# An attention, MLP and mixture-of-experts kernel: weights ahead of keys and values in the opening, and two set-ups moved to the third weight quarter

## Chip, cores and metric

The kernel runs on one core of one Trainium2 chip. The metric is the device time of one execution in microseconds (us). A core has five engines that each work through a queue of their own in a fixed order: TensorE (PE: matrix products), VectorE (DVE), ScalarE (ACT), GpSimd (POOL), and SyncE (SP), which here only issues DMA transfers. They wait for each other by semaphores.

## The reference

```
kv  = einsum('bhsd,bhse->bhde', k, v)            # 8 batches, 8 heads, 576 positions, 64 wide
out = einsum('bhsd,bhde->bhse', q, kv)
x   = out / sqrt(mean(out*out, -1) + 1e-6) * g_norm      # 4608 tokens x 512
h   = x @ w_in                                   # w_in 512 x 2048
y   = (max(h, 0) + alpha * min(h, 0)) @ w_out    # w_out 2048 x 512
e   = argmax(y @ w_gate)                         # 8 experts; one per token
result = softmax(y @ w_gate)[e] * sigmoid(y @ w_output_gate)[e] * (relu(y @ w1[e]) @ w2[e])
```

The weights w_in, w_out, alpha and the two gate matrices arrive as inputs of the launch; w_in and w_out are 64-bit floats in memory, which the kernel reads as pairs of 32-bit integers.

## The kernel before

**Tiles and stages.** The 4608 tokens form 12 blocks of 3 tiles of 128 tokens. For each block the attention makes the three tiles of x; `h` multiplies x by w_in (16 groups f of 128 columns), ScalarE copies the product out scaled as `m`, VectorE applies alpha (`r`), ScalarE makes the 16-bit `g`, and `y` multiplies g by w_out. All products use 16-bit halves: a number is a high half plus a low half, so that each product is three matmuls. Afterwards a router (`l`) chooses each token's expert, and the rest of the program is the experts' products.

**The opening.** x needs kv, which needs all keys and values of a batch. `load_kv_first` fetches batch 0's k and v as two large transfers (into the room of later w_in tiles, which is why the profile names them wi), `load_q` a pair of query tiles; `kvps` are the key-value products, `qps`/`ops` the query transposes and products, and per tile t of block b a chain of small VectorE instructions ends in the line that writes the low half of x (L352 before, L354 after), whose transpose by DMA ("x<-x") TensorE's `h` waits for. The tiles of block 1 are tiles 3 to 5, so that its last is `x_0_5`.

**Weights while they arrive.** The first two blocks run through w_in and w_out in four quarters j, while the raw weights are loaded. A quarter of either matrix is GF = 4 raw tiles of 512 KB, and five raw tiles can be held at a time. Each is loaded (`Dense.load`, L414: `rawwi`, `rawwo`), then built to 32 bits (`Dense.build`: ScalarE's absolute value at L433, and on VectorE L434, L437, L439, L441), which also collects a maximum; when a quarter's four are built, `scale_in(j)` or `scale_out(j)` turns the maximum over all partitions into a power of two. That takes two small TensorE products (`all_max`: `allmaxwi`, `allmaxwo`, L132 and L137) with VectorE steps between and behind them, and then the tiles are split into the 16-bit halves (L455 on ScalarE, L456 on VectorE; `scol` and `sogs` are the scales, which depend on g_norm and alpha). A list `prep` holds these steps, and `prep_steps(n)` takes n of them at the places where the code calls it:

```
while prep:
    prep_steps(1)
    step(attq)
    step(attq)
drain(attq)
```

Here `step(attq)` takes one step of the attention of block 0 (first the four `kv_step`s of batch 0).

**What sets the order.** The code is handed to a scheduler that reorders each engine's instructions ahead of the run by its own estimate of the times, under the dependences; the order on every engine is then fixed. `tc.keep_in_program_order(t)` forbids it to place the instruction t on its engine ahead of those that the code wrote earlier. SP issues a DMA only when the one eight issues earlier has landed, so that at most eight are under way.

**Constants.** `lst` (the experts' token lists) is filled by eight transfers of a tile `dmy`; `wgr` holds both gate matrices, whose maximum `gam` gives a scale `swg`, and whose halves `wg16` the router uses.

Of the kernel before, what the change touches and what calls it, by code (L numbers as in the profile page):

```python
# [20 lines left out]
P = 128  # L21
# [38 lines left out]
def body(ctx: ExitStack, tc, q, k, v, g_norm, w_in, w_out, alpha, w_gate, w_og, w1, w2, out):  # L60
# [49 lines left out]
    def pow2(am, nm, out_s, out_inv, top=14, wide=False):  # L110


        e = small.tile([P, am.shape[1]], I32, tag="pw_e", name="pw_e" + nm, padded_shape=[P, E])
        dve.tensor_scalar(out=e, in0=am.bitcast(I32), scalar1=0x7FF00000 if wide else 0x7F800000, scalar2=None,
                          op0=ALU.bitwise_and)
        if wide:
            dve.tensor_scalar(out=e, in0=e, scalar1=float((896 + top + 1) << 20), scalar2=float((896 + 254) << 20),
                              op0=ALU.max, op1=ALU.min)
            dve.tensor_scalar(out=out_inv.bitcast(I32), in0=e, scalar1=8.0, scalar2=float(-((896 + top) << 23)),
                              op0=ALU.mult, op1=ALU.add)  # L120
        else:
            dve.tensor_scalar(out=out_inv.bitcast(I32), in0=e, scalar1=float((top + 1) << 23),
                              scalar2=float(-(top << 23)), op0=ALU.max, op1=ALU.add)
        dve.tensor_scalar(out=out_s.bitcast(I32), in0=out_inv.bitcast(I32), scalar1=-1.0, scalar2=float(254 << 23),
                          op0=ALU.mult, op1=ALU.add)
# [93 lines left out]
    def load_kv_first():  # L219
        for nm, src, w in (("k", k, wi[:, 6:11]), ("v", v, wi[:, 11:16])):  # L220
            t = w.rearrange("p a t f -> p (a t f)").bitcast(F32)
            m = t[:, 0:H * QJ * D].rearrange("p (h j d) -> p h j d", h=H, j=QJ)
            r = t[0:SR, H * QJ * D:H * (QJ + 1) * D].rearrange("p (h d) -> p h d", h=H)
            sp.dma_start(out=m, in_=src[0, :, 0:QJ * P, :].rearrange("h (p j) d -> p h j d", j=QJ))
            sp.dma_start(out=r, in_=src[0, :, QJ * P:S, :].rearrange("h p d -> p h d"))
            kv_in[nm + "r", 0] = r
            for n in range(NPAIR):
                kv_in[nm, n] = m[:, 2 * n:2 * n + 2]

    def kv_step(n):  # L230
        b, hp = kv_order[n]
        kk, vv = kv_in.pop(("k", n)), kv_in.pop(("v", n))
        kr, vr = kv_in["kr", b], kv_in["vr", b]

        if hp % 2 == 0:
            kv_ps[b] = ps_a.tile([P, 2, D], F32, tag="a", name=f"kvps_{b}_{hp}")
        ps = kv_ps[b]
        for j in range(QJ + 1):
            for i in range(2):
                x, y = (kr[:, 2 * hp + i, :], vr[:, 2 * hp + i, :]) if j == 0 else (kk[:, i, j - 1, :], vv[:, i, j - 1, :])  # L240
                pe.matmul(ps[64 * i:64 * i + 64, hp % 2, :], x, y, start=(j == 0), stop=(j == QJ))
        if hp % 2 == 1:
            for i in range(2):
                sl = slice(64 * i, 64 * i + 64)
                dve.tensor_copy(out=kvbd[b % 2][sl, hp - 1:hp + 1, sl], in_=ps[sl])
        load_kv(n + 2 if n >= NPAIR else n + NPAIR if n < 2 else len(kv_order))
# [142 lines left out]
    def split(dst_h, dst_l, src, s):  # L389
        act.activation(out=dst_h, in_=src, func=AF.Copy, scale=s)  # L390
        dve.scalar_tensor_tensor(out=dst_l, in0=src, scalar=s, in1=dst_h, op0=ALU.mult, op1=ALU.subtract)  # L391
# [161 lines left out]
    def step(gens):  # L553
        while gens:
            if next(gens[0], "end") != "end":
                return
            gens.pop(0)
# [478 lines left out]
    def load_next():  # L1036
        if order:
            d, i = order.pop(0)
            d.load(i)

    load_kv_first()
    load_q(0, True)
    for _ in range(5):
        load_next()
    load_q(1, True)
    for half in range(2):
        sp.dma_start(out=gp[64 * half:64 * half + 64, :], in_=g_norm.rearrange("(p o) -> p o", o=1))
    gm = small.tile([P, 1], F32, tag="amx", name="gm")
    dve.tensor_scalar(out=gm, in0=gp, scalar1=-1.0, scalar2=None, op0=ALU.mult)
    dve.tensor_tensor(out=gm, in0=gm, in1=gp, op=ALU.max)  # L1050
    pow2(all_max(gm, "g"), "g", sg, isg, top=0)
    dve.tensor_tensor(out=gp, in0=gp, in1=sg, op=ALU.mult)
    al = small.tile([NF, P], F32, tag="al", name="al")
    sp.dma_start(out=al, in_=alpha.rearrange("(f p) -> f p", p=P))
    alp = ps_l.tile([P, NF], F32, tag="l", name="alp")
    pe.transpose(alp, al, ident[:NF, :NF])
    dve.tensor_copy(out=alphat, in_=alp)
# [27 lines left out]
    def prep_out(j):  # L1085
        return ([partial(build, dout, i) for i in range(j * GF, (j + 1) * GF)] + [partial(scale_out, j)]
                + [partial(dout.split, i) for i in range(j * GF, (j + 1) * GF)])
# [3 lines left out]
    def prep_steps(n):  # L1091
        for _ in range(n):
            if prep:
                prep.pop(0)()

    while prep:
        prep_steps(1)
        step(attq)
        step(attq)
    drain(attq)  # L1100
    for load in late:
        load()
    late = None
    dmy = small.tile([P, RT], I32, name="dmy", bufs=1)
    pool.memset(dmy, DUMMY)
    for e in range(E):
        sp.dma_start(out=lst.rearrange("(e p c) o -> e p (c o)", e=E, p=P)[e], in_=dmy)

    wgr = small.tile([P, NC, 2, E], F32, tag="wgr", name="wgr", bufs=1)
    sp.dma_start(out=wgr[:, :, 0, :], in_=w_gate.rearrange("(c p) e -> p c e", p=P))  # L1110
    sp.dma_start(out=wgr[:, :, 1, :], in_=w_og.rearrange("(c p) e -> p c e", p=P))
    gam = small.tile([P, 1], F32, tag="amx", name="gam")
    dve.tensor_reduce(out=gam, in_=wgr.rearrange("p c t e -> p (c t e)"), axis=AX.X, op=ALU.max,
                      apply_absolute_value=True)
    swg = small.tile([P, 1], F32, tag="swg", name="swg")
    pow2(all_max(gam, "wg"), "wg", swg, kl)
    for c in range(NC):
        split(wg16[:, c, 0, :], wg16[:, c, 1, :], wgr[:, c].rearrange("p t e -> p (t e)"), swg)

    def h_then_attention(i):  # L1120
        emit_h_block(i)
# [11 lines left out]
    attq.append(att_steps(1))  # L1133
    for j in range(NG):
        prep.extend(prep_out(j))
        if j == 0:
            drain(attq)
            h_part(0, j, gts[0])
            prep_steps(len(prep))
            y_part(0, j, gts[0], accs[0])  # L1140
            drain(attq)
            prep.extend(prep_in(1))
            h_part(1, j, gts[1])
        else:
            h_part(0, j, gts[0])
            if j == NG - 1:
                xt.pop(0)
                attq.append(att_steps(2))
            h_part(1, j, gts[1])
            prep_steps(len(prep))  # L1150
            if j < NG - 1:
                prep.extend(prep_in(j + 1))
            if j == NG - 1:
                xt.pop(1)
            y_part(0, j, gts[0], accs[0])
        if j == NG - 1:
            yq.append(lambda: route_1(0, *first[0]))
        y_part(1, j, gts[1], accs[1])
        prep_steps(len(prep))
# [72 lines left out]
```

## Time and profile before

| what | value |
|---|---|
| three executions, median (lowest to highest) | 1452.66 us (1451.47 to 1453.32) |
| the profiled execution: its own time, and its span | 1451.28 us, 1449.5 us |
| its mean granted clock of TensorE | 0.958 of full speed |
| TensorE busy | 1323.1 us, 91% of the span |
| VectorE busy | 836.9 us, 58% |
| ScalarE busy | 568.1 us, 39% |
| GpSimd busy | 333.9 us, 23% |

The span runs from the first to the last record of the profile; what the execution's own time has beyond it is 1.8 us. A busy share is a mean over stages: in the first 100 us TensorE waits much, later it hardly does.

### The profile page before, as it was taken

How to read it: one execution, taken by the hardware profiler on the slowest of the kernel's cores; microseconds unless marked ns; L12 is line 12 of the kernel's file. 1: busy time of each engine (PE TensorE's matmuls, PEld its weight loads, DVE VectorE, ACT ScalarE, POOL GpSimd, SP SyncE). 2: the span in 40 equal slices, each digit the busy share in tenths (PEclk: the TensorE clock that was granted, in tenths of full speed). 3: DMA queues.
4: the chain of work that ended last, by engine and by line, in shares of the span. 5: the costliest groups of instructions: out<-in, count | busy, mean ns of one | idle time of the engine just before them, and what ended most of it. 6: DMA issues, size and time to landing. Idle time of an engine off the chain costs nothing. (4 is left out here: it accounts for less than half of the span.)

```text
span 1449.5 us, 22268 instructions
## 1 busy us (share of the span) xinstructions
PE 1323.1 (91%) x7586; PEld 678.5 (47%) x7586; DVE 836.9 (58%) x2428; ACT 568.1 (39%) x937; POOL 333.9 (23%) x329
## 2 busy tenths in 40 slices
PE   4679985799999989999999999999789979999998
PEld 3435543445555545555555555544334434443443
DVE  5999877668786968788786876535012111211221
ACT  3365543346464646555555555411111111111111
POOL 2023334122132422212122222021212211211211
PEclk9589997899999989999999999999999999999999
DMA  9944047668595747686856663169996897689774
GB/s 255 280 113 144 1 118 152 81 131 210 142 269 123 212 121 175 189 218 197 168 160 136 198 154 96 23 163 128 291 260 134 223 252 198 135 215 215 141 152 139
DMA packets 347571, 243.25 MB, mean 168 GB/s; under 512 B 267692, under 2 KB 300476, under 8 KB 342464
## 3 DMA queue, kind: packets, MB, share of 16 engines
q1 hardware_dynamic: 330528, 206.11, 60.8%
q0 software_dynamic: 7712, 18.92, 4.2%
q10 hardware_dynamic: 9216, 16.78, 3.5%
q8 instruction: 60, 0.98, 0.3%
q14 instruction: 55, 0.45, 0.1%
HBM read 248.86 MB, written 53.97 MB: 209 GB/s over the span
## 5 line engine op out<-in xcount | busy, mean ns | idle before, releaser
L581 PE MATMUL h<-x,wi 128*128 128x384 f16 x2304 | 418.3, 334 | 12.1 <-DMA x<-x 5.8
L600 PE MATMUL y<-wo,g 128*128 128x512 f16 x1728 | 407.8, 383 | 12.4 <-ACT g L588 7.2
L581 PEld LDWEIGHTS <-wi 128*128 128x128 f16 x2304 | 224.9, 100 | 173.4 <-issue 22.6
L600 PEld LDWEIGHTS <-g 128*128 128x128 f16 x1728 | 164.9, 98 | 196.4 <-issue 8.5
L1009 DVE CAST h_d<-br_d 128x512 f16<-128x512 f32 x74 | 31.8, 430 | 332.4 <-DMA hT_d<-h_d 234.3
L1003 PE MATMUL bh_d<-lane,byT_d 128*128 128x512 f16 x888 | 201.3, 383 | 10.2 <-DMA lane<-ws 10.2
L1024 PE MATMUL bo_d<-lane,hT_d 128*128 128x512 f16 x888 | 200.5, 383 | 10.2 <-DMA hT_d<-h_d 10.0
L588 ACT CAST g<-r 128x384 f16<-128x384 f32 x192 | 97.4, 509 | 131.6 <-DVE r L586 125.5
L1003 PEld LDWEIGHTS <-byT_d 128*128 128x128 f16 x888 | 87.5, 99 | 118.6 <-issue 16.6
L1024 PEld LDWEIGHTS <-hT_d 128*128 128x128 f16 x888 | 87.2, 99 | 118.7 <-DMA hT_d<-h_d 13.3
L586 DVE SCALAR_TENSOR_TENSOR r<-m,alphat 128x384 f32<-128x384 f32 x192 | 123.1, 642 | 22.6 <-ACT m L584 18.1
L329 POOL TENSOR_TENSOR rs<-ms,mhalf 128x8 f32<-128x8 f32 x36 | 67.4, 1874 | 226.7 <-DVE qm L332 223.2
L1007 ACT ACTIVATE br_d<-bh_d 128x512 f32<-128x512 f32 x74 | 44.2, 597 | 177.3 <-PE bh_d L1003 138.9
L584 ACT ACTIVATE m<-h,scal 128x384 f32<-128x384 f32 x160 | 91.6, 574 | 40.5 <-PE h L581 37.3
L589 DVE TENSOR_TENSOR g<-r,g 128x384 f16<-128x384 f32 x160 | 92.9, 582 | 24.0 <-ACT g L588 21.4
L391 DVE SCALAR_TENSOR_TENSOR wlo_w<-rawe,es_w,whi_w 128x1024 f16<-128x1024 f32 x64 | 85.4, 1349 | 27.6 <-ACT whi_w L390 17.3
L1027 ACT ACTIVATE ob_d<-bo_d,msc_d 128x512 f32<-128x512 f32 x37 | 25.4, 687 | 165.1 <-PE bo_d L1024 160.6
L390 ACT ACTIVATE whi_w<-rawe,es_w 128x1024 f16<-128x1024 f32 x64 | 71.2, 1142 | 42.7 <-DMA ws<-whi_w 22.6
L521 ACT ACTIVATE eab_w<-rawe 128x1024 bf16<-128x1024 f32 x64 | 67.2, 1056 | 49.5 <-DMA rawe<-in_moe_w_dram 46.1
L1028 POOL DMA_INDIRECT out_dram<-ob_d,idx_d x37 | 38.5, 1040 | 193.8 <-ACT ob_d L1027 163.6
L726 POOL DMA_INDIRECT lst<-ids,pos x36 | 37.5, 1041 | 171.7 <-DVE pos L723 107.6
L352 POOL TENSOR_TENSOR x<-xs,x 128x512 f16<-128x512 f32 x30 | 46.9, 1563 | 110.7 <-ACT x L351 81.9
(297 smaller groups left out, 1288.9 us busy)
## 6 DMA issues: line engine op xcount, KB each, us to landing
lane<-ws SPq DMA_DIRECT2D x150, 1024.0 KB
rawe<-in_moe_w_dram SPq DMA_DIRECT2D x64, 512.0 KB
ws<-whi_w ACTq DMA_DIRECT2D x64, 256.0 KB
ws<-wlo_w SPq DMA_DIRECT2D x64, 256.0 KB
ytab<-row SPq DMA_DIRECT2D x32, 256.5 KB
q<-in_q_dram SPq DMA_DIRECT2D x16, 512.0 KB
rawwi<-in_moe_w_in_dram SPq DMA_DIRECT2D x16, 512.0 KB
rawwo<-in_moe_w_out_dram SPq DMA_DIRECT2D x16, 512.0 KB
```

Source lines behind the costliest of these rows:

```text
L329: pool.tensor_tensor(out=rs, in0=ms, in1=mhalf, op=ALU.pow)
L390: act.activation(out=dst_h, in_=src, func=AF.Copy, scale=s)
L391: dve.scalar_tensor_tensor(out=dst_l, in0=src, scalar=s, in1=dst_h, op0=ALU.mult, op1=ALU.subtract)
L521: act.activation(out=ab.rearrange("p a b -> p (a b)"), in_=raws[4 * m + i], func=AF.Abs)
L581: pe.matmul(ps, wi[:, f // 4 * NC + c, w, fs], xt[i][:, xc, :], start=(n == 0), stop=(n == 3 * NC - 1))
L584: act.activation(out=r0, in_=ps, func=AF.Copy, scale=(scst if start else scal)[:, f:f + 1])
L586: dve.scalar_tensor_tensor(out=r, in0=r0, scalar=alphat[:, f:f + 1], in1=r0, op0=ALU.mult, op1=ALU.max)
L588: act.copy(out=hi, in_=r)
L589: (pool if start else dve).tensor_tensor(out=lo, in0=r, in1=hi, op=ALU.subtract)
L600: pe.matmul(ps, g[:, t, f % GF, us], wo[:, f, w, :], start=(start and m == 0), stop=(stop and m == 2))
L1003: pe.matmul(hp, j["yT"][:, x, :], w1_[:, w, c, hs], start=(m == 0), stop=(m == 3 * NC - 1))
L1024: pe.matmul(po, hT[:, g, :], w2_[:, w, f, :], start=(m == 0), stop=(m == 3 * NFE - 1))
```

## The change

Five things are moved. In the opening, the four raw tiles of the first quarter of w_in, then g_norm (`gp`) and alpha (`al`), are loaded ahead of keys, values and queries. Ahead of the first `kv_step`, the code now writes the four builds and `scale_in(0)`, and only the four splits remain for the loop, which takes one step of the attention per step of `prep` where it took two. The first key-value product is kept in program order on TensorE. The filling of the lists and the set-up of the gate weights become a function that is called at j == 2. And at j == 0 the attention of block 1 is no longer drained ahead of `h_part(0, 0, ...)`. No instruction's work is changed. Lines after L241 stand 2 lower down in the changed kernel, until L1040.

```diff
--- before.py
+++ after.py
@@ -238,7 +238,9 @@
         for j in range(QJ + 1):
             for i in range(2):
                 x, y = (kr[:, 2 * hp + i, :], vr[:, 2 * hp + i, :]) if j == 0 else (kk[:, i, j - 1, :], vv[:, i, j - 1, :])
-                pe.matmul(ps[64 * i:64 * i + 64, hp % 2, :], x, y, start=(j == 0), stop=(j == QJ))
+                t = pe.matmul(ps[64 * i:64 * i + 64, hp % 2, :], x, y, start=(j == 0), stop=(j == QJ))
+                if (n, j, i) == (0, 0, 0):
+                    tc.keep_in_program_order(t)
         if hp % 2 == 1:
             for i in range(2):
                 sl = slice(64 * i, 64 * i + 64)
@@ -1038,20 +1040,21 @@
             d, i = order.pop(0)
             d.load(i)
 
+    for _ in range(GF):
+        load_next()
+    for half in range(2):
+        sp.dma_start(out=gp[64 * half:64 * half + 64, :], in_=g_norm.rearrange("(p o) -> p o", o=1))
+    al = small.tile([NF, P], F32, tag="al", name="al")
+    sp.dma_start(out=al, in_=alpha.rearrange("(f p) -> f p", p=P))
     load_kv_first()
     load_q(0, True)
-    for _ in range(5):
-        load_next()
+    load_next()
     load_q(1, True)
-    for half in range(2):
-        sp.dma_start(out=gp[64 * half:64 * half + 64, :], in_=g_norm.rearrange("(p o) -> p o", o=1))
     gm = small.tile([P, 1], F32, tag="amx", name="gm")
     dve.tensor_scalar(out=gm, in0=gp, scalar1=-1.0, scalar2=None, op0=ALU.mult)
     dve.tensor_tensor(out=gm, in0=gm, in1=gp, op=ALU.max)
     pow2(all_max(gm, "g"), "g", sg, isg, top=0)
     dve.tensor_tensor(out=gp, in0=gp, in1=sg, op=ALU.mult)
-    al = small.tile([NF, P], F32, tag="al", name="al")
-    sp.dma_start(out=al, in_=alpha.rearrange("(f p) -> f p", p=P))
     alp = ps_l.tile([P, NF], F32, tag="l", name="alp")
     pe.transpose(alp, al, ident[:NF, :NF])
     dve.tensor_copy(out=alphat, in_=alp)
@@ -1093,29 +1096,31 @@
             if prep:
                 prep.pop(0)()
 
+    prep_steps(GF + 1)
     while prep:
         prep_steps(1)
-        step(attq)
         step(attq)
     drain(attq)
     for load in late:
         load()
     late = None
-    dmy = small.tile([P, RT], I32, name="dmy", bufs=1)
-    pool.memset(dmy, DUMMY)
-    for e in range(E):
-        sp.dma_start(out=lst.rearrange("(e p c) o -> e p (c o)", e=E, p=P)[e], in_=dmy)
-
-    wgr = small.tile([P, NC, 2, E], F32, tag="wgr", name="wgr", bufs=1)
-    sp.dma_start(out=wgr[:, :, 0, :], in_=w_gate.rearrange("(c p) e -> p c e", p=P))
-    sp.dma_start(out=wgr[:, :, 1, :], in_=w_og.rearrange("(c p) e -> p c e", p=P))
-    gam = small.tile([P, 1], F32, tag="amx", name="gam")
-    dve.tensor_reduce(out=gam, in_=wgr.rearrange("p c t e -> p (c t e)"), axis=AX.X, op=ALU.max,
-                      apply_absolute_value=True)
-    swg = small.tile([P, 1], F32, tag="swg", name="swg")
-    pow2(all_max(gam, "wg"), "wg", swg, kl)
-    for c in range(NC):
-        split(wg16[:, c, 0, :], wg16[:, c, 1, :], wgr[:, c].rearrange("p t e -> p (t e)"), swg)
+
+    def constants():
+        dmy = small.tile([P, RT], I32, name="dmy", bufs=1)
+        pool.memset(dmy, DUMMY)
+        for e in range(E):
+            sp.dma_start(out=lst.rearrange("(e p c) o -> e p (c o)", e=E, p=P)[e], in_=dmy)
+
+        wgr = small.tile([P, NC, 2, E], F32, tag="wgr", name="wgr", bufs=1)
+        sp.dma_start(out=wgr[:, :, 0, :], in_=w_gate.rearrange("(c p) e -> p c e", p=P))
+        sp.dma_start(out=wgr[:, :, 1, :], in_=w_og.rearrange("(c p) e -> p c e", p=P))
+        gam = small.tile([P, 1], F32, tag="amx", name="gam")
+        dve.tensor_reduce(out=gam, in_=wgr.rearrange("p c t e -> p (c t e)"), axis=AX.X, op=ALU.max,
+                          apply_absolute_value=True)
+        swg = small.tile([P, 1], F32, tag="swg", name="swg")
+        pow2(all_max(gam, "wg"), "wg", swg, kl)
+        for c in range(NC):
+            split(wg16[:, c, 0, :], wg16[:, c, 1, :], wgr[:, c].rearrange("p t e -> p (t e)"), swg)
 
     def h_then_attention(i):
         emit_h_block(i)
@@ -1133,8 +1138,9 @@
     attq.append(att_steps(1))
     for j in range(NG):
         prep.extend(prep_out(j))
+        if j == 2:
+            constants()
         if j == 0:
-            drain(attq)
             h_part(0, j, gts[0])
             prep_steps(len(prep))
             y_part(0, j, gts[0], accs[0])
```

On SP, in the first transfers of the program, before:

```order
L224 DMA wi<-in_k_dram 128x8x256
L225 DMA wi<-in_k_dram 64x8x64
L224 DMA wi<-in_v_dram 128x8x256
L225 DMA wi<-in_v_dram 64x8x64
L212 DMA q_0_193<-in_q_dram 128x8x128
L414 DMA rawwi_195<-in_moe_w_in_dram 128x1024
L414 DMA rawwi_197<-in_moe_w_in_dram 128x1024
L414 DMA rawwi_199<-in_moe_w_in_dram 128x1024
L414 DMA rawwi_201<-in_moe_w_in_dram 128x1024
L414 DMA rawwo_203<-in_moe_w_out_dram 128x1024
L212 DMA q_2_205<-in_q_dram 128x8x128
```

and now:

```order
L416 DMA rawwi_189<-in_moe_w_in_dram 128x1024
L416 DMA rawwi_191<-in_moe_w_in_dram 128x1024
L416 DMA rawwi_193<-in_moe_w_in_dram 128x1024
L416 DMA rawwi_195<-in_moe_w_in_dram 128x1024
L1046 DMA gp<-in_g_norm_dram 64x1 x2
L1048 DMA al<-in_moe_alpha_dram 16x128
L224 DMA wi<-in_k_dram 128x8x256
L225 DMA wi<-in_k_dram 64x8x64
L224 DMA wi<-in_v_dram 128x8x256
L225 DMA wi<-in_v_dram 64x8x64
L212 DMA q_0_205<-in_q_dram 128x8x128
L416 DMA rawwo_207<-in_moe_w_out_dram 128x1024
```

The four rawwi and the two small transfers went from behind k, v and the first q to the front of the queue; the first rawwo stands behind k, v and q as before.

On VectorE, around the last tile of block 1's x (`x_0_5`; `cwo`, `cwi` and `uwi` are steps of builds, `wi<-wo` and `wo<-wi` splits), before:

```order
L441 SCALAR_TENSOR_TENSOR wi<-rawwo_937,cwo_1141 128x512
L352 TENSOR_TENSOR x_0_4_689<-xs_4_672,x_0_4_689 128x512
L347 TENSOR_TENSOR xs_5_709<-ops_5_704,rs_5_715 128x512
L437 TENSOR_SCALAR cwo_1197<-uwo_1194 128x512
L441 SCALAR_TENSOR_TENSOR wi<-rawwo_965,cwo_1169 128x512
L117 TENSOR_SCALAR pw_ewo_1231<-pw_ewo_1231 128x1
L456 SCALAR_TENSOR_TENSOR wi<-wo,scol,wi 128x512 x2
L437 TENSOR_SCALAR cwi_1329<-uwi_1326 128x512
L456 SCALAR_TENSOR_TENSOR wi<-wo,scol,wi 128x512 x2
L439 SCALAR_TENSOR_TENSOR cwo_1197<-rawwo_993,cwo_1197 128x512
L352 TENSOR_TENSOR x_0_5_726<-xs_5_709,x_0_5_726 128x512
L119 TENSOR_SCALAR isog<-pw_ewo_1231 128x1
```

and now:

```order
L349 TENSOR_TENSOR xs_5_854<-ops_5_849,rs_5_860 128x512
L136 TENSOR_SCALAR amdiagwi_1365<-ident,amrowwi_1363 1x1
L458 SCALAR_TENSOR_TENSOR wi<-wo,scol,wi 128x512
L479 TENSOR_SCALAR sogs<-sgn,sog 128x4
L458 SCALAR_TENSOR_TENSOR wi<-wo,scol,wi 128x512
L485 TENSOR_TENSOR em<-em,eg 128x1
L458 SCALAR_TENSOR_TENSOR wi<-wo,scol,wi 128x512 x2
L114 TENSOR_SCALAR pw_ewi_1368<-allmaxwi_1361 128x1
L354 TENSOR_TENSOR x_0_4_834<-xs_4_817,x_0_4_834 128x512
L354 TENSOR_TENSOR x_0_5_871<-xs_5_854,x_0_5_871 128x512
L487 TENSOR_TENSOR egd_1204<-eg,em 128x1
```

Ahead of `x_0_5` there were 17 rows of L434 and 15 of L441, and there are now 25 of the former (L436 there) and 20 of the latter (L443); the two tiles x_0_4 and x_0_5, which stood nine rows apart, stand one behind the other.

On TensorE, where the maximum of the last quarter of w_out (`allmaxwo_1968`) is spread to all partitions, before:

```order
L581 MATMUL h_15_1921<-x_358,wi 128x384
L581 LDWEIGHTS wi
L581 MATMUL h_15_1921<-x_358,wi 128x384
L581 LDWEIGHTS wi
L581 MATMUL h_15_1921<-x_358,wi 128x384
L137 MATMUL allmaxwo_1968<-amdiagwo_1972,ones_70 128x1
L581 LDWEIGHTS wi
L581 MATMUL h_12_1947<-x_582,wi 128x384
```

and now:

```order
L602 MATMUL y_2_1_1721<-wo,g_176 128x512
L602 LDWEIGHTS g_176
L602 MATMUL y_2_1_1721<-wo,g_176 128x512
L602 LDWEIGHTS g_176
L602 MATMUL y_2_1_1721<-wo,g_176 128x512
L137 MATMUL allmaxwo_1968<-amdiagwo_1972,ones_70 128x1
L583 LDWEIGHTS wi
L583 MATMUL h_11_1663<-x_660,wi 128x384
```

That product stood behind the last `h` of block 0 (h_15), and it now stands ahead of h_11 of block 1, some 200 rows of the queue earlier.

## Rows read from the trace of the kernel before

**Rows 1.** The page: the span, and busy time by engine.

```profile
span 1449.5 us, 22268 instructions
...
PE 1323.1 (91%) x7586; PEld 678.5 (47%) x7586; DVE 836.9 (58%) x2428; ACT 568.1 (39%) x937; POOL 333.9 (23%) x329
```

**Rows 2.** Stretches: span, busy us of PE, PEld, DVE, ACT, POOL; clock; DMA share, GB/s.

```profile
15.50:98.40 82.90, 56.57 (x344) 37.77 (x344) 75.58 (x258) 39.40 (x70) 17.50 (x12) 0.71 0.80 208
...
18.00:20.00 2.00, 1.41 (x12) 0.89 (x8) 2.00 (x6) 0.87 (x2) 0.00 (x0) 1.00 1.04 375
...
30.00:32.00 2.00, 0.00 (x1) 0.00 (x0) 1.72 (x6) 1.49 (x3) 1.57 (x1) 1.00 0.30 41
```

**Rows 3.** SP's timeline, opening: start, duration, line, transfer issued.

```profile
6.90 4.02 SPq L414 DMA_DIRECT2D rawwi<-in_moe_w_in_dram  x4
10.96 0.43 SPq L414 DMA_DIRECT2D rawwo<-in_moe_w_out_dram  x1
...
12.34 5.06 SPq L1047 DMA_DIRECT2D gp<-in_g_norm_dram  x2
...
25.31 4.62 SPq L1107 DMA_DIRECT2D lst<-dmy  x6
```

**Rows 4.** ScalarE's timeline, opening; brackets: idle time before, and what ended it.

```profile
16.50 0.67 ACT L433 ACTIVATE uwi<-rawwi 128x512 f32<-128x512 f32 x1 [0.62 <-DMA rawwi<-in_moe_w_in_dram]
17.85 0.67 ACT L433 ACTIVATE uwi<-rawwi 128x512 f32<-128x512 f32 x1 [0.68 <-DMA rawwi<-in_moe_w_in_dram]
...
21.93 0.67 ACT L433 ACTIVATE uwo<-rawwo 128x512 f32<-128x512 f32 x1 [1.15 <-DVE cwi L437]
```

**Rows 5.** TensorE's timeline, opening.

```profile
12.46 5.91 PE L241 MATMUL kvps<-wi 64*64 64x64 f32 x80 [12.46 <-DMA wi<-in_v_dram]
...
68.04 1.48 PE L581 MATMUL h<-x,wi 128*128 128x384 f16 x4
...
101.50 8.76 PE L581 MATMUL h<-x,wi 128*128 128x384 f16 x36 [4.37 <-DMA x<-x]
```

**Rows 6.** VectorE's timeline: first work, one tile's build, block 1's last x.

```profile
15.57 0.59 DVE L245 COPY kvbd<-kvps 64x128 f32<-64x128 f32 x2 [12.83 <-PE kvps L241]
16.19 0.69 DVE L434 TENSOR_SCALAR_CACHE_REDUCE uwi<-uwi 128x512 f32<-128x512 f32 x1
...
17.38 0.69 DVE L439 SCALAR_TENSOR_TENSOR cwi<-rawwi,cwi 128x512 int32<-128x512 int32 x1
...
97.66 0.67 DVE L352 TENSOR_TENSOR x<-xs,x 128x512 f16<-128x512 f32 x1
```

**Rows 7.** TensorE's timeline around the last quarter of w_out.

```profile
197.65 0.59 PE L600 MATMUL y<-wo,g 128*128 128x512 f16 x2 [1.60 <-ACT wo L455]
198.65 2.16 PE L600 MATMUL y<-wo,g 128*128 128x512 f16 x6 [0.41 <-DVE wo L456]
200.61 3.13 PE L581 MATMUL h<-x,wi 128*128 128x384 f16 x12
...
206.16 2.11 PE L581 MATMUL h<-x,wi 128*128 128x384 f16 x12
```

**Rows 8.** ScalarE's timeline, the same place.

```profile
196.88 1.33 ACT L455 ACTIVATE wo<-rawwo,sogs 128x512 f16<-128x512 f32 x2 [2.44 <-DVE sogs L477]
```

**Rows 9.** TensorE's timeline behind it.

```profile
215.87 0.27 PE L132 MATMUL allmaxkv<-ident,kvam 128*8 128x128 f32 x1 [0.83 <-DVE kvam L254]
218.62 0.38 PE L137 MATMUL allmaxkv<-amdiagkv,ones 8*128 8x8 f32 x2 [2.48 <-DVE amdiagkv L136]
222.94 0.40 PE L676 MATMUL l<-wg,yT 128*128 128x32 f16 x8 [3.93 <-DMA yT<-row]
```

**Rows 10.** VectorE's timeline in that stretch.

```profile
205.05 4.56 DVE L524 TENSOR_TENSOR eam_w<-eam_w,eab_w 128x512 bf16<-128x512 bf16 x5
```

**Rows 11.** GpSimd's and TensorE's timelines, far from the opening.

```profile
496.49 9.08 POOL L352 TENSOR_TENSOR x<-xs,x 128x512 f16<-128x512 f32 x1 [6.90 <-ACT x L351]
...
514.87 2.31 PE L600 MATMUL y<-wo,g 128*128 128x512 f16 x5 [5.54 <-ACT g L588]
```

## The prediction

> **What bounds the kernel now.** Over the whole span TensorE is the bound: it is busy for 91% of 1449.5 us [rows 1]. The change lies in the first hundred microseconds, where that doesn't hold: between 15.5 and 98.4 TensorE is busy for 56.6 of 82.9 us and VectorE for 75.6 [rows 2]. So I read next what TensorE's opening waits for. Its key-value products begin at 12.46, when v has landed; its first product with w_in comes at 68.04; and block 1's first `h` at 101.50 has 4.4 us of idle time before it, ended by the transposed x [rows 5]. The instruction that makes this x is VectorE's at 97.66 [rows 6], and the transfer and its start take the 3.2 us behind it. From there to 196.05 TensorE's timeline shows no hole of a microsecond, so **the time of `x_0_5` sets when the dense part really starts**, and VectorE's queue sets `x_0_5`. The next hole is at 197.65: 1.60 us for a split of w_out's last quarter, and 0.41 for the next [rows 7]. Behind it come three larger ones, 0.83, 2.48 and 3.93 us, until the router's first product at 222.94 [rows 9]; the first two are released by VectorE, and the third by a transpose of what VectorE wrote.
>
> **Transfers.** The opening is limited by bandwidth: at 18 to 20 us the DMA engines are full with 375 GB/s [rows 2]. Raw tiles reach ScalarE 1.35 us apart, each awaited for 0.6 to 0.7 us [rows 4]. Four of them put ahead of k and v thus delay k, v and q by some 5.4 us, and the key-value products begin near 17.9. But keys, values, one pair of queries, four raw tiles of w_in and one of w_out are the same set in either order, so the first raw tile of w_out lands when it did. The third raw tile was there at 17.85, so the fifth, w_out's, at 17.85 + 2 × 1.35 = 20.6; ScalarE took it only at 21.93, after 1.15 us in which it waited for VectorE [rows 4]. VectorE's first step on it can thus begin at about 21.4. That step stands in VectorE's new order right behind the four builds and the scale, ahead of the first copy of a key-value product.
>
> **How much lead VectorE gains.** Now its first work is at 15.57, when the first key-value product is there [rows 6]. One build takes 1.2 us from L434 to L439, and L439 and L441 fill 0.6 each before the next can start [rows 6], together 2.4, or 2.2 where nothing is late. Four are 9.2; some thirty small steps for g_norm, alpha and the scale add 2.0. So 11.2 us of work lie ahead of 21.4. Whether VectorE starts them at 5 or at 8, it has finished before and waits. Before the change it had done 5.8 us of work by then (from 15.57). **The lead is 5.4 us**, not the ten that its first instruction moves.
>
> **What now stands ahead of x_0_5.** The order has 8 more L434, 6 more L437, 7 more L439 and 5 more L441 ahead of it, and four gate splits fewer. At 0.69, 0.4, 0.6 and 0.6 us, that is 5.5 + 2.4 + 4.2 + 3.0 = 15.1; four gate splits of 0.16 and smaller steps take 0.6 off: **14.5 us**. Against it stands the idle time inside the stretch, 82.9 − 75.6 = 7.3 us [rows 2]. Part of it comes from late raw tiles of w_out: SP spends 4.62 us at 25.31 on list fills that wait for earlier ones [rows 3], while the DMA engines carry 41 GB/s [rows 2]. In the new order the tiles of w_out stand ahead of the fills. I let 3.5 of the 7.3 us go, half of it; the ends are none and all. So x_0_5, and with it h of block 1, come 14.5 − 5.4 − 3.5 = **5.6 us later**, from 1.8 (no idle time left) to 9.1 (all of it left). This is the change's cost: VectorE does the builds of later quarters ahead of the x that TensorE waits for. The x of block 0 comes at about the same time as before, since its wait for the split of w_in is replaced by one for x.
>
> **What comes back.** The builds that were done early are missing later, so VectorE is further ahead by the last quarter. The product that spreads w_out's last maximum stands ahead of h_11 of block 1 instead of behind h_15 of block 0, so the scale that ScalarE awaited for 2.44 us at 196.88 [rows 8] is there early: **−2.0 us** (1.60 + 0.41), at worst 0. The twelve `h` behind that hole took 3.13 us at half clock, and twelve of the same kind 2.11 at 206.16 [rows 7]: **−1.0**, between 0 and −1.5.
>
> The Trainium skill (TensorE: Matmul & The Clock Gate, What's actually happening) has the clock fall after a stretch without activity. Two waits of 1.60 and 0.41 us with products between them are hardly such a stretch, and if by that rule the fall has another cause the 1.0 us would not come back; no other row here settles it.
>
> At 205.05 VectorE spends 4.56 us on five maxima of expert weights [rows 10], in front of the work on which the holes at 215.87, 218.62 and 222.94 depend. In the new order seven such steps stand earlier, where TensorE has enough to do: 5.5 us of VectorE's queue, against 7.2 us of holes [rows 9]. I take **−3.5**, between 0 and −5.5, because the first products in this stretch also wait for ScalarE and for transposes.
>
> The gate weights and lists cost nothing where they now stand: by order the fills remain among the opening's transfers, and the router needs the gate halves only at 222.94.
>
> **Sum.** 5.6 − 2.0 − 1.0 − 3.5 = −0.9 us on the profiled execution's 1451.28 us (1.8 over its span). It is 1.4 below the median of 1452.66, to which I apply the same difference: **1451.8 us**. The ends are 1.8 − 2.0 − 1.5 − 5.5 = −7.2 (1445.5) and +9.1 (1461.8). The measurement tells 0.2%, or 2.9 us, from no change.
>
> **Rivals.** *Nothing is given back* (slower). The delay of x_0_5 stays and the late gains don't come, since transposes and ScalarE's queue end the waits around 222 instead of VectorE: +5.6, 1458.3 us. It counts as slower once less than 2.7 us comes back. For it speaks that the 3.93 us hole ends with a DMA; against it that the transpose is issued only when VectorE's row is written.
>
> *VectorE has no gaps any more* (faster). With all 7.3 us of idle time gone, x_0_5 is only 1.8 late, and with the gains at their middle values the sum is 1.8 − 6.5 = −4.7, 1448.0 us. For it speaks that raw tiles now come in the order in which VectorE takes them; against it that several of its steps wait for TensorE's maxima, which stand between products of h and y.
>
> *A far hole moves* (faster). At 514.87 TensorE has 5.54 us of idle time, in a chain that goes back to one GpSimd instruction of 9.08 us at 496.49 [rows 11], long after the change. TensorE's order differs in places until about 550 us; if this meeting of instructions is broken up, the sum is −0.9 − 5.5 = −6.4, 1446.3 us. A new one could arise as well, so its chance is small.
>
> **Numbers.** The forecast (within 0.2%) gets 0.42, nothing given back 0.25, no gaps 0.23, the far hole 0.10. Faster is then 0.33, same 0.42, slower 0.25. A range from 1446 to 1459 holds the rivals' centres and leaves out the outermost ends, which need every bound at once.
>
> **What the profile after would show.** Right: VectorE's first build near 6 us, a wait of some microseconds before 21.4, key-value products at 17 to 19, block 1's first `h` at 103 to 111, no wait for a split of w_out near 197, and the row of the router's first product at most 2 us from 222.9. Wrong: if VectorE doesn't wait for w_out's tile (then the lead is up to 9 us), if a TensorE maximum stalls VectorE between 80 and 105, or if the key-value products, rather than builds, hold up VectorE after 22.

## The result, and the profile after

The changed kernel is slower: 1469.2 us median (1466.32 to 1471.42, 4 runs) beside 1452.99 (1451.47 to 1458.46), a ratio of 1.0096 with a 95% interval of 1.0072 to 1.012 (the quotient of the two medians, 1.0112, lies inside it). Forecast was 1451.8 us. The profiled execution took 1467.59 us; its page begins, against [rows 1], with

```profile
span 1465.9 us, 22269 instructions
...
PE 1312.9 (90%) x7586; PEld 673.8 (46%) x7586; DVE 843.8 (58%) x2428; ACT 569.7 (39%) x937; POOL 335.5 (23%) x329
```

so that its span is 16.4 us longer. TensorE's timeline of the changed kernel says where, against [rows 5, 9]:

```profile
19.90 5.91 PE L241 MATMUL kvps<-wi 64*64 64x64 f32 x80
...
77.22 6.89 PE L583 MATMUL h<-x,wi 128*128 128x384 f16 x24 [5.96 <-DMA x<-x]
...
116.42 6.09 PE L583 MATMUL h<-x,wi 128*128 128x384 f16 x24 [4.70 <-DMA x<-x]
...
153.66 3.47 PE L602 MATMUL y<-wo,g 128*128 128x512 f16 x10 [3.71 <-POOL g L591]
...
235.93 0.38 PE L137 MATMUL allmaxkv<-amdiagkv,ones 8*128 8x8 f32 x2 [4.02 <-DVE amdiagkv L136]
...
236.57 0.37 PE L678 MATMUL l<-wg,yT 128*128 128x32 f16 x8 [0.26 <-DVE qm L337]
```

The key-value products begin 7.4 us later, block 0's first `h` 9.2 later, block 1's first `h` at 116.42 instead of 101.50, **14.9 us later**, and the router's first product 13.6 later. The first `h` of block 2 stands at 262.50 instead of 246.70 (15.8), and the end is 16.4 us later. So nearly as much as is lost at the end, 14.9 of 16.4 us, is there at the first `h` of block 1. Of the holes of [rows 7], those at 197.65 and 198.65 are gone and with them the half clock behind them; a new one of 3.71 us stands at 153.66. VectorE's timeline shows how x came to be late, against [rows 6]:

```profile
5.92 0.69 DVE L436 TENSOR_SCALAR_CACHE_REDUCE uwi<-uwi 128x512 f32<-128x512 f32 x1 [3.17 <-ACT uwi L435]
...
22.99 0.69 DVE L436 TENSOR_SCALAR_CACHE_REDUCE uwo<-uwo 128x512 f32<-128x512 f32 x1 [2.63 <-ACT uwo L435]
...
42.18 0.69 DVE L324 TENSOR_REDUCE st<-xs 128x8 f32<-128x512 f32 x1 [1.35 <-ACT xs L322]
...
44.98 0.69 DVE L436 TENSOR_SCALAR_CACHE_REDUCE uwi<-uwi 128x512 f32<-128x512 f32 x1 [1.32 <-ACT uwi L435]
...
75.56 0.69 DVE L436 TENSOR_SCALAR_CACHE_REDUCE uwi<-uwi 128x512 f32<-128x512 f32 x1 [2.38 <-ACT uwi L435]
...
81.87 0.62 DVE L588 SCALAR_TENSOR_TENSOR r<-m,alphat 128x384 f32<-128x384 f32 x1 [1.30 <-ACT m L586]
...
90.46 1.33 DVE L441 SCALAR_TENSOR_TENSOR cwi<-rawwi,cwi 128x512 int32<-128x512 int32 x1
...
94.09 1.40 DVE L354 TENSOR_TENSOR x<-xs,x 128x512 f16<-128x512 f32 x1
...
111.23 1.27 DVE L354 TENSOR_TENSOR x<-xs,x 128x512 f16<-128x512 f32 x2
```

VectorE starts at 5.92 and not at 15.57, waits 2.63 us for ScalarE's step on the first raw tile of w_out, and writes block 1's last two x from 111.23 on, the second of them, `x_0_5`, at 111.83 (97.66 before). The stretches of the changed kernel, in the columns of [rows 2], give the sum:

```profile
5.90:112.50 106.60, 55.69 (x385) 37.59 (x385) 93.58 (x293) 45.35 (x77) 18.58 (x12) 0.78 0.79 213
5.90:22.90 17.00, 6.07 (x52) 4.43 (x54) 12.34 (x45) 3.77 (x6) 0.00 (x0) 1.00 1.09 297
66.00:77.20 11.20, 4.16 (x21) 3.60 (x22) 8.75 (x24) 2.12 (x4) 2.08 (x1) 0.65 1.05 221
195.00:225.00 30.00, 29.85 (x171) 15.77 (x168) 21.85 (x49) 18.54 (x31) 11.41 (x11) 1.00 0.38 108
```

From its first work to the end of x_0_5 VectorE is busy for 93.6 of 106.6 us, where it was for 75.6 of 82.9. Its start is 9.6 us earlier, its work 18.0 us more and its idle time 5.7 us more: `x_0_5` is some 14 us late, 14.2 by its two rows. Its transpose and start took 0.7 us longer than before, which makes the 14.9.

### The profile page after: what moved, and what is told of

The parts are those of the page before. It is cut to its first block, busy times and chain, and to the rows that moved or that the text cites. A ratio compares the mean times of both kernels' runs of the same rounds, so it can differ in the third digit from the quotient of the medians.

```text
span 1465.9 us, 22269 instructions
## 1 busy us (share of the span) xinstructions
PE 1312.9 (90%) x7586; PEld 673.8 (46%) x7586; DVE 843.8 (58%) x2428; ACT 569.7 (39%) x937; POOL 335.5 (23%) x329
## 5 line engine op out<-in xcount | busy, mean ns | idle before, releaser
L583 PE MATMUL h<-x,wi 128*128 128x384 f16 x2304 | 414.0, 331 | 21.5 <-DMA x<-x 12.0
L591 DVE TENSOR_TENSOR g<-r,g 128x384 f16<-128x384 f32 x160 | 94.1, 588 | 24.4 <-ACT g L590 22.8
L879 POOL DMA_INDIRECT yg<-ytab,idx_d x37 | 39.1, 1058 | 129.5 <-issue 89.3
```

What stands on the lines that cost most here:

```text
L583: pe.matmul(ps, wi[:, f // 4 * NC + c, w, fs], xt[i][:, xc, :], start=(n == 0), stop=(n == 3 * NC - 1))
L591: (pool if start else dve).tensor_tensor(out=lo, in0=r, in1=hi, op=ALU.subtract)
```

## Experiments

One theory (A) is that the drain which was removed costs the time: without it, the builds of later quarters stand ahead of block 1's x on VectorE. The rival (B) is that the opening costs it: with raw weights ahead of k and v, everything that needs x starts later. The marks of each run's profile are in this table; "first h" is TensorE's first product of w_in for that block, "384th h" the start of the timeline's row, of some 12 products, that completes two blocks' worth, "router" the first `l`. Each ratio is to the kernel before on the same chip, with its 95% interval; the kernel before itself had medians of 1450 to 1455 us on these chips.

| run | first h, block 0 | first h, block 1 | 384th h | router | ratio |
|---|---|---|---|---|---|
| before | 68.0 | 101.5 | 206.2 | 222.9 | |
| e9 before again | 65.9 | 99.3 | 203.9 | 220.7 | one run |
| changed | 77.2 | 116.4 | 223.2 | 236.6 | 1.0096 (1.0072 to 1.012) |
| e1 changed, drain back | 66.2 | 92.6 | 203.7 | 222.8 | 1.0057 (1.003 to 1.0085) |
| e2 before, no drain | 64.7 | 115.0 | 217.7 | 237.5 | 1.0226 (1.0169 to 1.0282) |
| e3 before, loads ahead | 70.5 | 90.9 | 200.9 | 221.6 | 0.9998 (0.9969 to 1.0027) |
| e4 before, constants moved | 65.6 | 95.3 | 203.9 | 220.8 | 1.0032 (1.0007 to 1.0057) |
| e5 changed, old loads | 90.0 | 121.1 | 221.5 | 235.4 | 1.0113 (1.0071 to 1.0156) |
| e6 opening as changed, rest old | 73.6 | 95.8 | 209.2 | 226.5 | 1.0094 (1.0059 to 1.0129) |
| e7 changed, thin builds | 70.4 | 104.0 | 206.4 | 224.9 | one run |
| e8 loads ahead, thin builds | 68.4 | 90.2 | 202.7 | 221.3 | one run |
| e10 loads ahead, constants moved | 71.0 | 92.9 | 204.7 | 221.5 | 0.9974 (0.9953 to 0.9996) |
| e11 e6 without the kept order | 70.7 | 92.8 | 204.3 | 216.9 | 0.9965 (0.9941 to 0.9989) |
| e12 e6 without early builds | 68.7 | 96.7 | 202.3 | 215.3 | 0.9953 (0.9929 to 0.9976) |
| e13 changed, no kept order | 67.4 | 108.7 | 216.4 | 232.5 | 1.0083 (1.0063 to 1.0103) |
| e14 changed, no early builds | 68.1 | 111.1 | 219.9 | 233.6 | 1.0091 (1.0056 to 1.0125) |
| e15 e14 with the drain back | 65.6 | 92.9 | 205.0 | 222.0 | 1.0005 (0.9986 to 1.0023) |
| e16 e12 again | 68.0 | 96.1 | 200.2 | 213.2 | 0.9955 (0.9938 to 0.9971) |

**e1, the drain put back into the changed kernel.**

```diff
         if j == 0:
+            drain(attq)
             h_part(0, j, gts[0])
```

> The changed kernel with the drain of block 1's attention put back ahead of h of block 0. Theory A (the removed drain costs the time: builds of later quarters now stand ahead of block 1's x on VectorE): in this order some 40 large VectorE instructions fewer stand ahead of x_0_5, about 25 us of its queue, so block 1's first h begins at 90 to 104 us instead of 116.4, and the time falls to 1449 to 1458 us. Theory B (the loads ahead of keys and values cost the time, since h of block 0 begins at 77.2 instead of 68.0): block 1's first h still begins 9 us later than before, at 110 or later, and the time stays at 1461 us or above.

Block 1's first `h` came at 92.6, 24 us earlier than in the changed kernel and inside the range of A. The time is between the theories: 1.0057, above A's range, and below the changed kernel. TensorE's timeline shows why being earlier than before wins little:

```profile
87.61 5.14 PE L602 MATMUL y<-wo,g 128*128 128x512 f16 x17
92.59 1.30 PE L583 MATMUL h<-x,wi 128*128 128x384 f16 x7
93.73 1.03 PE L602 MATMUL y<-wo,g 128*128 128x512 f16 x4
```

The `h` of block 1 now stands among `y` of block 0, which the kernel before had finished ahead of its 4.37 us hole [rows 5]. What could be won ahead of 101.5 is about that hole, whereas the changed kernel, late behind it, stayed late. That the run ends 0.6% above the kernel before is not explained by the opening, where its router's product is at the same place. The profiled execution took 1454.06 us, 6 less than the run's median, so its trace can't show the whole of it.

**e2, only the drain removed from the kernel before.**

```diff
         if j == 0:
-            drain(attq)
             h_part(0, j, gts[0])
```

> The kernel before with only the drain removed. Theory A: 26 large VectorE instructions more stand ahead of x_0_5, 16 us of queue; block 1's first h moves from 101.5 to 110 to 117, and the time rises by 7 to 15 us to 1460 to 1468. Theory B: the opening is as it was, and the time is within 3 us of 1453.

A holds: block 0's first `h` is even early, block 1's is 13.5 us late, with VectorE's last x and TensorE's wait for it just as in the changed kernel:

```profile
109.74 1.27 DVE L352 TENSOR_TENSOR x<-xs,x 128x512 f16<-128x512 f32 x2
```

```profile
114.98 3.38 PE L581 MATMUL h<-x,wi 128*128 128x384 f16 x10 [4.75 <-DMA x<-x]
```

The time is worse than A said, 2.3%, 33 us by the ratio. At the router's product 14.6 of them are there. The rest is lost later; one place is a hole of 5.82 us ahead of a router's product at 503.85, which waits for a transpose (0.30 us at 481.32 in the kernel before). Why it is late there is open.

**e3, only the loads ahead.**

```diff
+    for _ in range(GF):
+        load_next()
+    for half in range(2):
+        sp.dma_start(out=gp[64 * half:64 * half + 64, :], ...)
+    al = small.tile([NF, P], F32, tag="al", name="al")
+    sp.dma_start(out=al, in_=alpha.rearrange("(f p) -> f p", p=P))
     load_kv_first()
     load_q(0, True)
-    for _ in range(5):
-        load_next()
+    load_next()
     load_q(1, True)
-    for half in range(2):
-        sp.dma_start(out=gp[64 * half:64 * half + 64, :], ...)
...
-    al = small.tile([NF, P], F32, tag="al", name="al")
-    sp.dma_start(out=al, in_=alpha.rearrange("(f p) -> f p", p=P))
```

> The kernel before with only the order of the loads changed (raw w_in, g_norm and alpha ahead of keys, values and queries). Theory B: h of block 0 begins near 77 instead of 68 and the time rises by 7 to 10 us, to 1460 to 1463. Theory A: h of block 0 is late too, but x_0_5 stands right behind x_0_2 on VectorE (77 large instructions ahead of it, where there were 91), so that block 1's first h is late by 0 to 4 us only, and the time is 1450 to 1457.

B falls: block 0's first `h` is 2.4 us late and not 9, and the time is the same. A had block 1's first `h` 0 to 4 us late; it is 10.6 us early. By the order, 77 large VectorE instructions stand ahead of x_0_5 there, and 91 before: raw w_in early lets x move up as long as the drain keeps its place in the code.

**e4, only the constants moved.** Lists and gate weights become `constants()` as in the diff, on the kernel before.

```diff
+        if j == 2:
+            constants()
         if j == 0:
             drain(attq)
```

> The kernel before with only the lists and gate weights set up at the third quarter. Both theories: 8 large VectorE instructions fewer stand ahead of x_0_5, and the time is within 4 us of 1453, rather below it.

The opening's marks came 2 to 6 us earlier, but the time rose by 4.6 us by the ratio, just outside what was expected and on the other side. The profiled execution took 1467.26 us, 9 more than the run's median, so where that arises is open.

**e5, the changed kernel with the old loads.** The diff of e3 reversed, on the changed kernel.

> The changed kernel with the old order of the loads (keys, values and queries first), all else as changed. If the loads ahead cost the time (theory B), it falls to about 1460 us or below. If the removed drain costs it (theory A), block 1's first h stays at 112 to 125 us (x_0_5 has 117 large VectorE instructions ahead of it, as in the changed kernel, and they start later), and the time is 1467 to 1485 us.

As A said. Here the kept order shows its condition: with the old loads the key-value products wait on TensorE for maxima of weights that land later, begin at 31.37 instead of 19.90, and block 0's first `h` comes at 90. Yet block 1's is only 4.7 us later than in the changed kernel: VectorE's queue, not block 0, decides it.

**e6, only the opening.** The changed kernel with drain and constants as before.

```diff
+    constants()
...
-        if j == 2:
-            constants()
         if j == 0:
+            drain(attq)
```

> Only the opening as changed (loads, builds and the scale written ahead of the first key-value step, that step kept in program order); the drain and the constants as before. Theory A: block 1's first h at 88 to 96 us, the time within 5 us of the kernel before, since the nine us that TensorE starts earlier are lost again to waits for VectorE before 205 us. Theory B: 1460 us or more.

Block 1's first `h` fits A, the time fits B: 0.9% slower. So the opening has a cost of its own when the drain is there, and e11 and e12 ask which edit it belongs to.

**e7, thin builds in the changed kernel.**

```diff
+    fixed = small.tile([P, 1], I32, name="fixed", bufs=1)
+    pool.memset(fixed, 0x3C000000)
...
+            if i < GF:
                 a = cv.tile([P, 512], I32, ...)
                 dve.tensor_scalar(out=a, in0=u.bitcast(I32), ...)
                 dve.scalar_tensor_tensor(out=a, in0=hi, ...)
+            else:
+                a = fixed.to_broadcast([P, 512])
```

> The changed kernel with two of the four VectorE steps of a build left out for the weights behind the first quarter of either matrix (L439 and L441; a fixed bit pattern takes their place, so the weights are wrong and the output is not the reference's). Theory A: x_0_5 has 88 large instructions ahead of it instead of 117, some 14 us less, and block 1's first h begins at 99 to 106 us instead of 116.4. If transfers or TensorE's own maxima set that start, it stays at 112 us or later. The time of the whole is not compared, since other tokens go to other experts.

This takes away the suspected cost and leaves the drain out:

```profile
98.77 0.69 DVE L354 TENSOR_TENSOR x<-xs,x 128x512 f16<-128x512 f32 x1
...
99.71 0.67 DVE L354 TENSOR_TENSOR x<-xs,x 128x512 f16<-128x512 f32 x1
```

```profile
103.98 4.24 PE L589 MATMUL h<-x,wi 128*128 128x384 f16 x14 [1.55 <-DMA x<-x]
```

Block 1's first `h` is at 103.98, 12.4 us earlier than in the changed kernel, and the 384th `h` 16.8 earlier. Builds on VectorE ahead of x are what made x late.

**e8, thin builds with the loads alone.** The diffs of e3 and e7, on the kernel before.

> The kernel before with the loads changed as in the run with the loads alone, and the same two steps of the later builds left out (wrong weights). There block 1's first h began at 90.9 and the 384th h, which ends the dense part of the first two blocks, at 200.9 us. If VectorE's total work holds TensorE up between these two, block 1's first h begins at 80 to 88 us and the 384th h at 188 us or earlier. If TensorE itself is the bound there, the distance between the two stays at 110 us.

The first answer falls: with two steps fewer per build, nothing moved (90.2 and 202.7 beside 90.9 and 200.9). From there to the 384th `h` TensorE is the bound: it is busy for 108.2 of 112.5 us, and VectorE for 78.4. It agrees with e1: what block 1's first `h` gains ahead of some 97 us (101.5 less the hole) is hardly seen at the 384th.

**e9, the kernel before once more.** No edit.

> The kernel before, profiled once more, to see how far the marks of one kernel move from run to run: block 1's first h (101.5 us) and the 384th h (206.2 us) are expected within 1.5 us of the first profile, and what moves beyond that lies behind 260 us. If the marks move by 5 us or more, the differences of the other runs in the opening are scatter too.

The marks moved by 2.2 us together, more than the 1.5 expected; 1.1 of it is there at the first key-value product already, and the hole ahead of block 1's first `h` is 4.37 us in both. The end moved by 6.3 us. e12 and e16, one kernel again, differ by 0.6 to 2.1 us in the marks. So differences of 5 us and more in the opening are taken as real, and single profiles say less about what lies behind.

**e10, loads ahead and constants moved.** The diffs of e3 and e4.

> The kernel before with the loads ahead and the constants at the third quarter, without the other three edits. Each alone ended the dense part of the first two blocks earlier (200.9 and 203.9 us against 206.2). If the gains of the first 206 us last to the end, 1448 to 1453 us beside a kernel before of 1455; if what is won there is lost in the later order, 1453 to 1460.

The better of the two: 0.26% faster than the kernel before.

**e11 and e12, one edit of the opening left out.**

```diff
-                if (n, j, i) == (0, 0, 0):
-                    tc.keep_in_program_order(t)
```

is e11 against e6, and

```diff
-    prep_steps(GF + 1)
     while prep:
```

is e12 against e6.

> The opening as changed, but with the key-value products free to move ahead of the maxima on TensorE; drain and constants as before. If the wait of the key-value products behind the maxima of g_norm, alpha and w_in was the cost of the opening, the 384th h comes at 199 to 204 us instead of 209.2, as with the loads alone. If the builds written ahead are the cost, it stays at 207 to 211.

> The opening as changed, but without the five steps written ahead of the first key-value step; drain and constants as before. The other way round: 199 to 204 us for the 384th h if the builds written ahead are the cost of the opening, 207 to 211 if the kept order of the key-value products is.

Neither alternative was right: either edit alone is harmless. e12 is 0.47% faster than the kernel before, e11 0.35%; only both together cost 0.94%. Of that, 5 to 7 us show at the 384th `h`. More is lost far behind the opening. Block 2's first `h` of e6 comes at 249.29, only 2.6 us later than before (e12: 239.63), but between 400 and 540 us TensorE is busy for 124.7 us in e6, 132.4 in the kernel before and 130.6 in e12. Two holes of e6 against the same places of e12:

```profile
414.50 0.37 PE L132 MATMUL allmax_w<-ident,amx_w 128*1 128x128 f32 x1 [3.42 <-DVE amx_w L397]
...
494.57 0.40 PE L678 MATMUL l<-wg,yT 128*128 128x32 f16 x8 [5.68 <-DMA yT<-row]
```

```profile
404.00 0.38 PE L137 MATMUL allmax_w<-amdiag_w,ones 1*128 1x1 f32 x2 [1.71 <-DVE amdiag_w L136]
...
473.70 0.37 PE L678 MATMUL l<-wg,yT 128*128 128x32 f16 x8 [1.11 <-DMA yT<-row]
```

Why the opening's two edits together lengthen these waits is open.

**e13 and e14, the same edits left out of the whole change.** The diffs of e11 and e12, on the changed kernel.

> The whole change, but with the key-value products free to move ahead of the maxima on TensorE. If the two edits of the opening cost 10 to 15 us together wherever they stand, the time falls from +1.0% to about 0 to +0.4%. If the removed drain alone sets the time, block 1's first h stays at 112 to 118 us and the time at +0.8 to +1.3%.

> The whole change, but without the five steps written ahead of the first key-value step. As in the run before: 0 to +0.4% if the opening's pair is to blame, +0.8 to +1.3% and block 1's first h at 112 to 118 us if the removed drain is.

Both stay slow, 0.83 and 0.91%. Their first `h` of block 1, at 108.7 and 111.1, is earlier than the second alternative said. So without the drain the pair matters for 5 to 8 us of that mark, but hardly for the time.

**e15, e14 with the drain back; e16, e12 again.** The diff of e1 on e14; and no edit to e12.

> The whole change with the drain put back and without the early builds: loads ahead, kept order and the constants at the third quarter. Block 1's first h at 90 to 98 us. If the constants cost nothing, -0.3 to -0.6% as in the run without them; if they cost what they did beside the old opening (+0.3%), 0 to -0.2%.

> The kernel of the run e12 once more (loads ahead and kept order, drain and constants as before): -0.3 to -0.6% against the kernel before if its gain is real, within 0.2% if it was the chip.

Putting the drain back takes the ratio from 1.0091 to 1.0005, and the first `h` from 111.1 to 92.9. The time lies just above the 0 to -0.2% expected if the constants cost something, and its interval covers them. e16 repeats e12's gain: 0.9955 (0.9938 to 0.9971). It is the best kernel of this study: the kernel before with the loads ahead, the key-value products in program order, and one step of the attention per step of preparation. (One or two steps give the same order on every engine, in the changed kernel and in e6 alike.) Why the constants at the third quarter take that gain away again (e15), though beside the loads alone they did not (e10), is open.

## Why the prediction was wrong

**What bounds.** Right: x_0_5 set block 1's first `h`, and TensorE's wait before it ended with the transposed x in the changed kernel too.

**Transfers and lead.** Nearly right. The key-value products began at 19.90 and not at 17.9, just outside the 17 to 19 that were named as a sign, and ScalarE took the raw tile of w_out at 22.29, after a wait for the transfer, and not at 20.6:

```profile
22.29 0.67 ACT L435 ACTIVATE uwo<-rawwo 128x512 f32<-128x512 f32 x1 [0.30 <-DMA rawwo<-in_moe_w_out_dram]
...
74.88 0.66 ACT L435 ACTIVATE uwi<-rawwi 128x512 f32<-128x512 f32 x1 [4.94 <-DMA rawwi<-in_moe_w_in_dram]
```

VectorE's wait ahead of it was there. By 22.9 VectorE had worked for 12.3 us, and 7.1 before: a lead of 5.2 us, and 5.4 were forecast.

**The delay of x_0_5** is the step that failed: "So x_0_5, and with it h of block 1, come 14.5 − 5.4 − 3.5 = 5.6 us later". Its upper end was 9.1; `x_0_5` came 14.2 us later, and `h` 14.9. The mechanism was right, and two terms were mis-sized: the work was 18.0 us and not 14.5, and the idle time, of which 3.5 us were to go, grew by 1.3.

*Work.* The count of added instructions was right, but some took longer. Six VectorE instructions that ran beside GpSimd's took together 3.6 us more than others of their line, among them L441 with 1.33 us (0.69 at 7.11) and the x at 94.09 with 1.40 us (0.67 at 111.83). Before, it was 0.5 us in the same stretch. GpSimd's side of the last one:

```profile
93.58 1.36 POOL L591 TENSOR_TENSOR g<-r,g 128x384 f16<-128x384 f32 x1
```

*Idle time.* I let half of the 7.3 us go because w_out's tiles came ahead of the list fills. None went in sum. In the kernel before, all but 0.3 us of it lay behind 22.9, as its first stretch shows:

```profile
15.50:22.90 7.40, 5.93 (x53) 5.08 (x54) 7.14 (x19) 3.53 (x6) 0.00 (x0) 1.00 1.11 327
```

In the changed kernel 8.4 us lie behind 22.9, 1.3 us more:

```profile
22.90:112.50 89.60, 49.62 (x335) 33.16 (x335) 81.23 (x248) 41.58 (x72) 18.58 (x12) 0.74 0.74 198
```

The wait for w_out's tiles did shrink. It was

```profile
36.26 0.69 DVE L434 TENSOR_SCALAR_CACHE_REDUCE uwo<-uwo 128x512 f32<-128x512 f32 x1 [1.92 <-ACT uwo L433]
```

before, and is now two waits of 0.44 and 0.38 us. But others came in its place, in VectorE's timeline above: 1.32 and 2.38 us for tiles of w_in, and 1.35 and 1.30 us for steps of the attention and of block 0's `m`. So the sum would have been 18.0 − 5.2 + 1.3 = 14.1, and not 5.6.

The wait at 75.56 came because ScalarE had waited 4.94 us, until 74.88, for a raw tile of w_in. SP's timeline has that tile's load at 66.94, behind 8.70 us spent on three loads of w_out and behind later keys and values. Of the 8.70 us, SP's waits give 4.5 to VectorE's L443, the step of a build that reads a raw tile last and so frees its room. Late loads were in part VectorE's own lateness:

```profile
43.07 8.70 SPq L416 DMA_DIRECT2D rawwo<-in_moe_w_out_dram  x3
...
65.59 0.37 SPq L200 DMA_DIRECT2D k<-in_k_dram  x1
66.02 0.87 SPq L200 DMA_DIRECT2D v<-in_v_dram  x1
66.94 0.93 SPq L416 DMA_DIRECT2D rawwi<-in_moe_w_in_dram  x2
67.97 2.31 SPq L357 DMA_TRANSPOSE x<-x  x1
```

```profile
SPq L416 <- DVE wo L443: 4.5, 1, 4.5
```

Between 66 and 77.2 the DMA engines were full (share 1.05 in the stretches above). The same stretch of the kernel before had 0.70:

```profile
66.00:77.20 11.20, 10.16 (x55) 5.83 (x55) 10.35 (x34) 6.85 (x15) 0.54 (x1) 0.69 0.70 157
```

That goes with block 0's late first `h` too. Its last x was written at 67.24, 1.9 us later than before, near the "about the same time" of the prediction; but its transpose was issued from 67.97 on, and `h` began at 77.22, 9.3 us behind the end of x. In [rows 5, 6] 3.2 us lie between the end of x_0_5 and `h`, at a DMA share of 0.72 from 98.4 to 101.5. That the full DMA engines delayed the transpose was not tried alone.

**Which edit.** The text named the builds ahead of x, but costed the diff as one order and did not ask which line of code makes it. e2, e7 and the comparisons of e1 with the changed kernel and of e15 with e14 show that it is the removed drain that puts the builds ahead of x; with it, the same loads let x stand earlier than before. The time has a second cause, which the prediction did not ask for: e6, with the drain and block 1's first `h` at 95.8, is as slow as the whole change, and there the early builds and the kept order cost it together, part of it behind 400 us.

**What comes back.** The hole of 2.0 us and the half clock of 1.0 us were given back as forecast: between 195 and 225 TensorE is busy for 29.85 of 30 us at a granted clock of 1.00 (0.68 from 200.6 to 203.8 before), and the doubt about the 1.0 us was not borne out. Not foreseen was the hole at 153.66, behind one GpSimd instruction:

```profile
90.16 1.08 POOL L591 TENSOR_TENSOR g<-r,g 128x384 f16<-128x384 f32 x1 [1.18 <-ACT g L590]
...
144.32 0.92 POOL L591 TENSOR_TENSOR g<-r,g 128x384 f16<-128x384 f32 x1 [3.04 <-ACT g L590]
...
147.84 5.76 POOL L591 TENSOR_TENSOR g<-r,g 128x384 f16<-128x384 f32 x1 [2.60 <-ACT g L590]
```

It took 5.76 us where its like took 0.92, and TensorE lost 3.71 us and some more to the lower clock, granted at 0.73 in the mean from 153.66 to 160.00. In the tail, the three holes of [rows 9] shrank from 7.2 to 4.3 us (4.02 and 0.26 are left), near the 3.5 that I took; but by block 2's first `h` 2.2 us of that were lost again; the next `l`, at 246.50, waited 2.83 us for its transposes, and 1.58 before. So the gains were 2.0 + 1.0 + 3.0 and the new loss 3.7, which would leave 12.6 of the 14.9 at the router; 13.6 were measured, and the lower clock behind the new hole fits the rest.

**The rivals.** "Nothing is given back" had the sign and the wrong size, for the same reason. "No gaps any more" was refuted, as its own argument against it said: several steps waited for what others delivered. "A far hole moves" came true in its condition: the hole of 5.54 us at 514.87 [rows 11] is gone, with 1.63 us the longest near its place. But another grew, from 0.30 us at 481.32 to the first of these,

```profile
504.11 0.36 PE L678 MATMUL l<-wg,yT 128*128 128x32 f16 x8 [3.22 <-DMA yT<-row]
...
534.44 4.10 PE L583 MATMUL h<-x,wi 128*128 128x384 f16 x24 [1.63 <-ACT m L586]
```

and with smaller ones TensorE's holes from 400 to 545 us add up to 8.4 us, where they were 7.6. Nothing was gained there.

## What to carry to other kernels

Removing a call that has the code write the next stage's instructions early (a drain) can move the instruction that the next stage needs behind work that is not urgent, once a scheduler has fixed the order. Look for the instruction that ends the critical engine's wait, and count what stands ahead of it, edit by edit. In the changed kernel lateness behind such a mark stayed, while being up to 11 us early at it won at most some 6 us at the 384th `h`. Idle time in a stretch should be kept in the sum unless the very instructions that wait are shown to be released earlier: one wait shrank here, and others took its place. Edits that are each harmless can cost together, far behind the place that they change.

## What the runs showed of the hardware

Some instructions of VectorE and GpSimd that ran side by side took much longer than their like: VectorE's L441 1.33 us at 90.46 (0.69 in [rows 6], where it is L439) while GpSimd worked (from 90.16), and GpSimd's L591 5.76 us at 147.84 while VectorE was busy for 5.0 of the 5.8 us. Not every such meeting was slow: L591 took 0.92 us at 144.32, and VectorE worked then as well. The Trainium skill (SBUF — State Buffer, Who interferes with whom) says that VectorE instructions with two inputs from SBUF and GpSimd instructions that read SBUF contend for a read interface, and that the order of issue decides who waits. The trace agrees in that L441 has two such inputs, that during the 0.92 us VectorE mostly ran L436, which reads one tile, and that either side was the slow one. The two inputs don't cover L122, which reads one tile and took 0.88 us at 88.13 beside GpSimd, and 0.15 at 53.94. Which instruction held the other up was not tried.
